# Two tiles in place of one for T's first place and the mixed weights, and 0.8 in place of 0.5 for a head's transfer

## The chip, the cores and the metric

The kernel runs on one core of a Trainium2 chip. Time is device time of one execution in microseconds (us); lower is better. A core has five engines with a queue of instructions each: TensorE (PE, its weight loads are shown as PEld), VectorE (DVE), ScalarE (ACT), GpSimd (POOL) and SyncE (SP), which here only starts DMA transfers. Each engine works through its queue in order and stands still when its next instruction waits.

## The reference

Attention over 4 batches, 12 heads, 448 tokens and 64 columns, in which the heads are mixed before and after the softmax, and then a two-layer network over the 1792 tokens:

```python
scores = scale * np.matmul(q, k.transpose(0, 1, 3, 2))
scores = np.einsum('bhij,hg->bgij', scores, w_pre)
scores = scores - np.max(scores, axis=-1, keepdims=True)
attn = np.exp(scores)
attn = attn / (np.sum(attn, axis=-1, keepdims=True) + 1e-09)
attn = np.einsum('bhij,hg->bgij', attn, w_post)
return np.matmul(attn, v).astype(np.float32)
...
h = x @ w_in
g = h * np.clip(h + 3.0, 0.0, 6.0) / 6.0
return (g @ w_out).astype(np.float32)
```

## The kernel before, in words

The tokens of a batch are taken in eight halves m of 60 (the last of a batch smaller), 32 halves in all. For a half, the products of q and k for 12 heads are made in three steps of four heads (`scores`, line 432). ScalarE copies each step's result from PSUM into one of two s buffers (line 457; the products go through one PSUM tile of two banks, `pair`). Then SyncE starts one transfer for each head (line 464), four for a step and twelve for a half (24 smaller ones in the last half of a batch). They turn the layout round: in T, the partitions are head and token, so that one matmul can mix the heads.

T has two places that alternate by half: even halves use the first 5376 columns of the tile AR, odd halves the tile T_one. From T the row products with w_pre are made (line 521), VectorE finds the maximum (529), ScalarE takes the exponential (530), GpSimd divides by the sum and splits the result into two 16-bit parts (539 to 542), and TensorE mixes the heads with w_post (558). Two engines write the mixed weights A into AR from column 6144 on: VectorE (567) and ScalarE (569). A has three slots in a ring there. From A and v come the attention outputs (603). The first layer of the network (801) fills in where it can, with its own evictions (814, 816). All of this is the first stage, to about 704 us; the second layer (1071) fills most of the rest. In the second stage AR holds weights and activations in two slots of 11520 columns (`wg`, `w_view`, `g_view`).

The order of all instructions is made ahead of time by a planner (`Plan`): each operation has an engine, an assumed time, what it reads and writes, and a priority; the planner plays the engines through, taking the operation of the best priority that is ready, tries 32 random variations and keeps the best. A DMA costs its engine the assumed time (0.5 for all of SyncE's), and lands later by its bytes. Where the plan sees TensorE idle near the start it puts matmuls without a result (line 839). The planner holds T's place and A for different buffers; the waits in the program are made afterwards, from tiles and what is read and written in them.

Of the kernel before, what the change touches and what calls it, by code (L numbers as in the profile page):

```python
# [11 lines left out]
F16 = mybir.dt.float16  # L12
BF16 = mybir.dt.bfloat16
F32 = mybir.dt.float32
# [12 lines left out]
P = 128  # L27
# [4 lines left out]
CU = 60  # L32
# [259 lines left out]
def body(ctx: ExitStack, tc: tile.TileContext, q4, kT, vj, wpre0, wpost0, ident0, w_in, w_out, outT):  # L292
    nc = tc.nc
    PE, ACT, DVE, POOL, SP = nc.tensor, nc.scalar, nc.vector, nc.gpsimd, nc.sync
# [4 lines left out]
    apool = ctx.enter_context(tc.tile_pool(name="apool", bufs=1))  # L299
# [9 lines left out]
    plan = Plan()  # L309
# [3 lines left out]
    def buf(pool, shape, dt, tag, name, bufs=1, ring=True):  # L313

        g = rings.setdefault((id(pool), tag), Ring(bufs)) if ring else None
        return Buf(lambda: pool.tile(shape, dt, tag=tag, name=name, bufs=bufs), g)

    def const(shape, dt, name, pool=keep):
        return Buf(lambda: pool.tile(shape, dt, name=name))

    def act(dur, fn, r, w, prio):
        return plan.op("ACT", dur, fn, r, w, prio)

    def dve(dur, fn, r, w, prio, share=False):
        return plan.op("DVE", dur, fn, r, w, prio, share=share)
# [4 lines left out]
    def pe(dur, fn, r, w, prio, after=(), mode=0):  # L330
        return plan.op("PE", dur, fn, r, w, prio, after, 0, mode)

    def dma(nbytes, fn, r, w, prio, after=()):
        return plan.op("SP", 0.5, fn, r, w, prio, after, nbytes)
# [22 lines left out]
    def place(places):  # L357
        z = Buf(None)
        z.pool = places
        return z  # L360
# [50 lines left out]
        qs[b, c] = t  # L411
        (bulk if b + c else dmas)(P * QX * 4, t, q4[b, c], [t], at, after)

    AR = const([P, 23424], F16, "AR", apool)
    T_one = const([P, 6, S], F32, "T_one", one)
    T_home = [lambda: AR()[:, :5376].bitcast(F32).rearrange("p (t j) -> p t j", t=6), T_one]
    T_zero = [Buf(None), T_one]
    a_ring = Ring(3)
    last_qk, last_av, Ts, Au = [], [], {}, {}

    def a_view():
        return AR()[:, 6144:].bitcast(F32).rearrange("p (x y) -> p x y", y=3 * CU)

    def products(q, half, ks_, p, at):

        def mm():
            for cc in range(2):
                pr = 2 * p + cc
                o = (6 * half + pr) * CU
                for u in range(2):  # L430
                    r = slice(u * D, u * D + D)
                    PE.matmul(at[u]()[cc * D:cc * D + D], q()[r, o:o + D], ks_[cc]()[r, pr % 3, :], start=True, stop=True)  # L432

        return mm

    def scores(m, p, at):
        b, n = divmod(m, 8)
        c, half = divmod(n, 2)
        if p == 0:
            Ts[m] = Buf(T_home[m % 2], rings.setdefault(("T", m % 2), Ring(1)))  # L440
        T, q = Ts[m], qs[b, c]
        ks_ = [ks[b, (2 * p + cc) // 3] for cc in range(2)]
        kr = [(ks_[cc], (2 * p + cc) % 3) for cc in range(2)]
        st = buf(wpool, [P, 2, S], F32, "x", f"s_{m}_{p}", X_BUFS) if m == 0 else buf(rot, [P, 2, S], F32, "s", f"s_{m}_{p}", 2)
        if m < 2 and (m or p):
            ps = [place(singles) for u in range(2)]
            at2 = [lambda u=u: ps[u]()[:, :S] for u in range(2)]
        else:
            two = place(pairs)
            ps = [(two, 0), (two, 1)]  # L450
            at2 = [lambda u=u: two()[:, u, :S] for u in range(2)]
        last_qk[:] = [pe(0.77, products(q, half, ks_, p, at2), [*kr, q], ps, at, last_qk, mode=1)]
        if m < 2:
            act(0.48, lambda: ACT.activation(st()[:, 0], at2[0](), AF.Copy), [ps[0]], [(st, 0)], at + 0.5)
            dve(0.57, lambda: DVE.tensor_copy(st()[:, 1], at2[1]()), [ps[1]], [(st, 1)], at + 0.5)
        else:
            act(0.9, lambda: ACT.activation(st(), two()[:, :, :S], AF.Copy), ps, [(st, 0), (st, 1)], at + 0.5)  # L457
        parts = [(0, 10, 6, 0)] if n < 7 else [(0, 10, 2, 0), (20, 5, 2, 2)]
        for cc in range(2):
            for u in range(2):  # L460
                h = 2 * (2 * p + cc) + u
                for q0, r, t, t0 in parts:
                    def go(cc=cc, u=u, h=h, q0=q0, r=r, t=t, t0=t0):
                        SP.dma_start(T()[4 + h:4 + h + 12 * (r - 1) + 1:12, t0:t0 + t], st()[D * cc + q0:D * cc + q0 + r * t, u, :])  # L464

                    dma(r * t * 2100, go, [(st, u), T_zero[m % 2]], [(T, (h, t0))], at + 0.7)


    vs = {}
# [32 lines left out]
    def step(s):  # L502
# [31 lines left out]
        if t == 0:  # L534
            Au[m] = Buf(a_view, a_ring)
# [312 lines left out]
    for m in range(2):  # L848
        for p in range(3):
            scores(m, p, -10 + 8 * m + 1.6 * p)  # L850
# [6 lines left out]
    for s in range(NS + 12):  # L857
# [5 lines left out]
        while todo and todo[0][0] - 2 <= s:  # L863
            at, m, p = todo.pop(0)
            if p == 0 and m % 2 == 0:
                queries(m // 8, m % 8 // 2, at - 5)
            scores(m, p, at)
# [13 lines left out]
        for C in range(16):  # L881
            b, c = divmod(C, 4)
# [28 lines left out]
    def minus(out, x, y, op, at, big, after=()):  # L911
        plan.op("DVE", 1.15, lambda: DVE.tensor_tensor(out(), x(), y(), op=op), [x, y], [out], at, after, share=True)

    WS, GP = {}, {}
    wg_ring = Ring(2)

    def wg(i):
        return Buf(lambda: AR()[:, 11520 * i:11520 * i + 11520], wg_ring)

    slots = [wg(i) for i in range(2)]  # L920
    t_last, a_last = last_pre[-5:-2], last_av[-4:]

    def w_view(t, z, i):
        return t()[:, :6144].rearrange("p (z m f c) -> p z m f c", z=2, m=3, f=8)[:, z, i // 2, 4 * (i % 2):4 * (i % 2) + 4]

    def g_view(t, at, z):
        return t()[:, at:at + 1792].rearrange("p (z f n) -> p z f n", z=2, f=4)[:, z]

    WS["P1"] = slots[0]

    def w_split(name, i, t, at, after):
        b = WS[name]
        split(View(t, lambda: t().rearrange("p (f c) -> p f c", f=4)), wo_r[int(name not in ("P1", "P2"))], lambda y: w_view(b, y, i), (b, (name, i)), 4 * P, at, after, False)

    def g_split(name, b, i, t, x, o, at, after):
        GP[name, b, i] = (lambda z: g_view(x, o, z)), (x, (name, b, i))
        split(t, g_s[b], lambda z: g_view(x, o, z), (x, (name, b, i)), 4 * NH, at, after, True)
# [69 lines left out]
    def g_tile(name):  # L1007
        return gbuf([P, 4, NH], F32, "gr", name, GR)

    def g_load(b, kk, half, i, at):  # L1010
        t = g_tile(f"g{kk}{half}_{b}_{i}_{at}")
        src, keys_ = g_rows(b, kk, half, i)
        load(458752, lambda: SP.dma_start(t(), src()), keys_, [t], at, [close_a])
        return t

    def g_put(name, b, i, t, at, home):
        after = [close_a]
        if home is None:
            ring = later_home.pop(0) if name not in ("P1", "P2") and later_home else "gx"
            if ring == "gy":  # L1020
                after = [close_a, close_w]
            x = gbuf([P, 1792], F16, "gx", f"gx_{name}_{b}_{i}", GX) if ring == "gx" else wbuf([P, 1792], F16, "gy", f"gy_{name}_{b}_{i}", GY)
            home = x, 0
        x, o = home
        g_split(name, b, i, whole(t), x, o, at, after + (a_last if x is slots[1] else []))
# [10 lines left out]
    def g_two(b, at):  # L1036
        later_home[:] = ["gy"] * GY
        if b % 2:
            z = [wg(i) for i in range(2)]
        for i in range(2):  # L1040
            t = at + (6 if b else G2_BY) * i
            b12, b11, b22, b21 = g_load(b, 0, 1, i, t), g_load(b, 0, 0, i, t + 0.1), g_load(b, 1, 1, i, t + 0.2), g_load(b, 1, 0, i, t + 0.3)
            t1 = g_tile(f"t1_{b}_{i}")
            minus(t1, b12, b11, ALU.subtract, t + 1, True)
            minus(b11, b22, t1, ALU.subtract, t + 1.1, True)
            minus(b12, b22, b12, ALU.subtract, t + 1.2, True)
            minus(b21, b21, b11, ALU.subtract, t + 1.3, True)
            for j, (name, x) in enumerate((("P6", b11), ("P7", b12), ("P4", b21), ("P5", t1), ("P3", b22))):
                home = None
                if b % 2:  # L1050
                    n = 5 * i + j
                    home = z[n // 5], 1792 * (n % 5)
                g_put(name, b, i, x, t + 2 + j, home)

    u_t = {}
# [78 lines left out]
    for b in range(B):  # L1134
        g_two(b, 2000 + 1000 * b if b else G2_AT)
        stage2(b, 20000 + 1000 * b)
# [54 lines left out]
```

## Time and profile before

| | |
|---|---|
| median of 3 runs | 926.43 us (920.86 to 934.22) |
| profiled execution | 935.05 us, span of its instructions 933.3 us |
| mean granted TensorE clock | 0.936 |
| TensorE busy | 838.6 us (90%) |
| VectorE, ScalarE, GpSimd busy | 602.5, 529.7, 373.1 us |

Busy time is the time in which at least one instruction of an engine ran. The granted clock is a share of full speed: 1.00 is 2.4 GHz, 0.50 is 1.2 GHz. A line such as "L567 DVE" is line 567 of the kernel on VectorE; `AR<-single` is the tile written and the tile read.

### The profile page before, as it was taken

How to read it: one execution, taken by the hardware profiler on the slowest of the kernel's cores; microseconds unless marked ns; L12 is line 12 of the kernel's file. 1: busy time of each engine (PE TensorE's matmuls, PEld its weight loads, DVE VectorE, ACT ScalarE, POOL GpSimd, SP SyncE). 2: the span in 40 equal slices, each digit the busy share in tenths (PEclk: the TensorE clock that was granted, in tenths of full speed). 3: DMA queues.
4: the chain of work that ended last, by engine and by line, in shares of the span. 5: the costliest groups of instructions: out<-in, count | busy, mean ns of one | idle time of the engine just before them, and what ended most of it. 6: DMA issues, size and time to landing. Idle time of an engine off the chain costs nothing.

```text
span 933.3 us, 28114 instructions
## 1 busy us (share of the span) xinstructions
PE 838.6 (90%) x11599; PEld 661.4 (71%) x11599; DVE 602.5 (65%) x1185; ACT 529.7 (57%) x1043; POOL 373.1 (40%) x535
## 2 busy tenths in 40 slices
PE   8699997698798898898897898889899999999998
PEld 2356665455475675676575666567799999999998
DVE  4477584458565734877565597586457588898542
ACT  3357685467676755676666666678447475243110
POOL 3145686267774744565545446668200000000000
PEclk9779699789999998999988999899999999999999
DMA  6563543362534465554645656553449785463301
GB/s 211 187 188 119 157 137 120 93 216 92 176 104 132 120 203 185 173 176 144 196 122 188 199 178 199 173 159 92 122 131 356 221 264 173 124 185 113 100 25 46
DMA packets 100417, 146.98 MB, mean 157 GB/s; under 512 B 9824, under 2 KB 79552, under 8 KB 100288
## 3 DMA queue, kind: packets, MB, share of 16 engines
q1 hardware_dynamic: 100288, 145.17, 50.1%
q8 instruction: 91, 1.49, 0.7%
q14 instruction: 38, 0.31, 0.1%
HBM read 75.23 MB, written 31.20 MB: 114 GB/s over the span
## 4 chain that ended last, share of the span: by engine, by line
PE 51%; DMA 12%; DVE 10%; ACT 8%; SPq 7%; POOL 6%; issue 5%; ACTq 0%; DVEq 0%; POOLq 0%
PE single L1071 21%; PE single L801 13%; SPq L464 6%; DMA AR<-s 6%; PE single L558 5%; PE pair L432 4%; PE single L521 3%; POOL e L539 3%; DVE nb L529 3%; POOL el L542 3%; PE single L603 2%; ACT e L530 2%; ACT s L457 2%; DMA T_one<-s 2%; DMA wsd_P<-WF 2%
## 5 line engine op out<-in xcount | busy, mean ns | idle before, releaser
L801 PEld LDWEIGHTS <-wi 128*128 128x128 f16 x2304 | 217.3, 99 | 37.1 <-issue 28.9
L801 PE MATMUL single<-x,wi 128*128 128x208 f16 (+1 forms) x2304 | 233.3, 263 | 9.4 <-ACT AR L569 6.6
L542 POOL TENSOR_TENSOR el<-e,eh 128x448 f16<-128x448 f32 x156 | 172.3, 1119 | 87.9 <-ACT eh L541 85.6
L539 POOL TENSOR_SCALAR e<-e,r 128x448 f32<-128x448 f32 x180 | 132.2, 746 | 77.1 <-DVE r L533 69.7
L1071 PEld LDWEIGHTS <-ws_P 128*128 128x128 f16 x1440 | 138.0, 98 | 0.0
L530 ACT ACTIVATE e<-single,nb 128x448 f32<-128x448 f32 x180 | 113.0, 637 | 35.2 <-DVE nb L529 34.9
L432 PE MATMUL pair<-ks,qx 64*64 64x448 f32 x728 | 101.6, 627 | 27.7 <-ACT s L457 27.3
L567 DVE TENSOR_SCALAR AR<-single 128x480 f32<-128x480 f32 (+1 forms) x92 | 58.4, 641 | 95.6 <-DMA AR<-s 68.7
L529 DVE TENSOR_REDUCE nb<-single 128x1 f32<-128x448 f32 x180 | 102.5, 613 | 21.9 <-PE single L521 21.6
L569 ACT ACTIVATE AR<-single 128x480 f32<-128x480 f32 (+1 forms) x92 | 52.9, 582 | 100.1 <-DMA AR<-s 66.5
L457 ACT ACTIVATE s<-pair 128x896 f32<-128x896 f32 x90 | 82.3, 915 | 37.6 <-DMA T_one<-s 20.6
L541 ACT ACTIVATE eh<-e 128x448 f16<-128x448 f32 x156 | 87.0, 576 | 19.8 <-POOL e L539 18.7
L814 ACT ACTIVATE g<-single,three,uh 128x240 f32<-128x240 f32 (+1 forms) x128 | 68.2, 540 | 51.6 <-PE single L801 51.2
L603 PEld LDWEIGHTS single<-AR,v 128*64 128x64 f32 x1536 | 80.6, 144 | 22.5 <-DVE AR L567 6.3
L558 PEld LDWEIGHTS <-eh 60*128 60x128 f16 x2496 | 69.2, 101 | 34.4 <-issue 31.2
L603 PE MATMUL single<-AR,v 128*64 128x120 f32 (+1 forms) x1536 | 86.1, 273 | 6.6 <-DVE AR L567 6.2
L816 DVE SCALAR_TENSOR_TENSOR g<-g,six,single 128x240 f32<-128x240 f32 (+1 forms) x128 | 56.3, 442 | 53.4 <-ACT g L814 53.1
L558 PE MATMUL single<-wpost_h,eh 60*128 60x60 f16 x1248 | 76.6, 204 | 11.1 <-ACT e L530 5.4
L558 PE MATMUL single<-wpost_h,el 60*128 60x60 f16 x1248 | 75.6, 204 | 4.4 <-POOL el L542 4.4
L558 PE MATMUL single<-wpost_l,eh 60*128 60x60 f16 x1248 | 75.4, 204 | 0.0
L1071 PE MATMUL single<-gx_P,ws_P 128*128 128x224 f16 x720 | 69.3, 259 | 0.0
L1071 PE MATMUL single<-AR,ws_P 128*128 128x224 f16 x720 | 69.3, 259 | 0.0
(241 smaller groups left out, 1163.8 us busy)
## 6 DMA issues: line engine op xcount, KB each, us to landing
AR<-s SPq DMA_DIRECT2D x192, 105.0 KB
T_one<-s SPq DMA_DIRECT2D x144, 105.0 KB
wi<-in_w_in SPq DMA_DIRECT2D x16, 768.0 KB
wo<-in_w_out SPq DMA_DIRECT2D x24, 512.0 KB
wsd_P<-WF SPq DMA_DIRECT2D x42, 256.0 KB
wP<-wsd_P SPq DMA_DIRECT2D x36, 256.0 KB
gd<-g SPq DMA_DIRECT2D x32, 240.0 KB
gd<-g SPq DMA_DIRECT2D x32, 208.0 KB
```

Of the source, the lines that this page charges most:

```text
L432: PE.matmul(at[u]()[cc * D:cc * D + D], q()[r, o:o + D], ks_[cc]()[r, pr % 3, :], start=True, stop=True)
L457: act(0.9, lambda: ACT.activation(st(), two()[:, :, :S], AF.Copy), ps, [(st, 0), (st, 1)], at + 0.5)
L529: dve(0.53, lambda r=r: DVE.tensor_reduce(nb()[:, r:r + 1], ps[r]()[:, :S], axis=AX.X, op=ALU.max, negate=True), [ps[r]], [(nb, r)], s + 0 ...
L530: act(0.62, lambda r=r: ACT.activation(e()[:, r], ps[r]()[:, :S], AF.Exp, bias=nb()[:, r:r + 1], accum_out=sm()[:, r:r + 1]), [ps[r], (nb, ...
L539: pool(0.63, lambda r=r: POOL.tensor_scalar(e()[:, r], e()[:, r], rr()[:, r:r + 1], 1.0, op0=ALU.mult, op1=ALU.mult), [rr], [(e, r)], s + ...
L541: act(0.47, lambda r=r: ACT.activation(eh()[:, r], e()[:, r], AF.Copy), [(e, r)], [(eh, r)], s + 0.65 + 0.3 * r)
L542: pool(1.02, lambda r=r: POOL.tensor_tensor(el()[:, r], e()[:, r], eh()[:, r], op=ALU.subtract), [(e, r), (eh, r)], [(el, r)], s + 0.7 + 0 ...
L558: PE.matmul(out, x()[rows, r, js], z()[rows], start=(i == 0), stop=(i == len(mix) - 1))
L603: PE.matmul(ps()[u * D:(u + 1) * D, k:k + (n if p1 else CI)], v()[:, jc, g * D:(g + 1) * D], cols(jc * H + g), start=(jc == 0), stop=(jc = ...
L801: PE.matmul(pv(), wi_g[g]()[:, w, f0, cc, :], x()[:, z, cc, :n], start=(cc == 0 and i == 0), stop=(cc == 5 and i == 2))
L814: act(0.44, lambda fc=fc, pv=pv, r=r: ACT.activation(r(), pv(), AF.Relu, bias=three()[:, fc:fc + 1], scale=uh()[:, fc:fc + 1]), [ps, (thre ...
L1071: PE.matmul(ps()[:, :NH], w_view(w, y, 2 * m + i)[:, f], g(x)[:, f, :], start=(i == 0 and f == 0 and (y, x) == (0, 0)), stop=(i == 1 and f ...
```

## The change

AR loses its first 6144 columns to a tile of its own, T_two, and A now begins at column 0 of AR. The second stage's two slots are made of pieces of both tiles; a tile's parts are found by `x[at // 6144]`, and of the ten places for g the third and later of a slot move by 768 columns. In the planner a head's transfer costs SyncE 0.8 in place of 0.5.

```diff
-    AR = const([P, 23424], F16, "AR", apool)
+    AR = const([P, 17280], F16, "AR", apool)
+    T_two = const([P, 6144], F16, "T_two", apool)
     T_one = const([P, 6, S], F32, "T_one", one)
-    T_home = [lambda: AR()[:, :5376].bitcast(F32).rearrange("p (t j) -> p t j", t=6), T_one]
+    T_home = [lambda: T_two()[:, :5376].bitcast(F32).rearrange("p (t j) -> p t j", t=6), T_one]
...
     def a_view():
-        return AR()[:, 6144:].bitcast(F32).rearrange("p (x y) -> p x y", y=3 * CU)
+        return AR()[:, :].bitcast(F32).rearrange("p (x y) -> p x y", y=3 * CU)
...
-                    dma(r * t * 2100, go, [(st, u), T_zero[m % 2]], [(T, (h, t0))], at + 0.7)
+                    plan.op("SP", 0.8, go, [(st, u), T_zero[m % 2]], [(T, (h, t0))], at + 0.7, (), r * t * 2100)
...
     def wg(i):
-        return Buf(lambda: AR()[:, 11520 * i:11520 * i + 11520], wg_ring)
+        return Buf(lambda: (AR()[:, 5376:11520], AR()[:, 11520:16896]) if i else (T_two(), AR()[:, :5376]), wg_ring)
...
     def w_view(t, z, i):
-        return t()[:, :6144].rearrange("p (z m f c) -> p z m f c", z=2, m=3, f=8)[:, z, i // 2, 4 * (i % 2):4 * (i % 2) + 4]
+        x = t()
+        return (x[0] if isinstance(x, tuple) else x[:, :6144]).rearrange("p (z m f c) -> p z m f c", z=2, m=3, f=8)[:, z, i // 2, 4 * (i % 2):4 * (i % 2) + 4]
 
     def g_view(t, at, z):
-        return t()[:, at:at + 1792].rearrange("p (z f n) -> p z f n", z=2, f=4)[:, z]
+        x = t()
+        if isinstance(x, tuple):
+            x, at = x[at // 6144], at % 6144
+        return x[:, at:at + 1792].rearrange("p (z f n) -> p z f n", z=2, f=4)[:, z]
...
-                    home = z[n // 5], 1792 * (n % 5)
+                    home = z[n // 5], 1792 * (n % 5) + (768 if n % 5 > 2 else 0)
```

Built with the two tiles alone, the program has every engine's instructions in the order of before, and only its waits differ; all that moves is moved by 0.8. The numbers in brackets below are semaphores: DMAHW0 to 7 are those of transfers, PE, DVE, Activation and Pool those of the engines.

VectorE, the first writes of A (line 567, in the change 568), near the start of the program; `vst` is a maximum over v, `WF` the decoding of weights. Before:

```order
L344 TENSOR_REDUCE vst_339<-v_266 128x1 [waits DMAHW0_49]
L567 TENSOR_SCALAR AR<-single_156 128x48x10 [waits DMAHW4_49,DMAHW5_49,DMAHW3_49,DMAHW6_49,DMAHW2_49,DMAHW7_49,DMAHW0_49,PE_49]
L533 RECIPROCAL r_375<-sm_337 128x2 [waits Pool_49]
L652 TENSOR_SCALAR WF,wist_380<-WF 128x768 [waits Activation_49]
L567 TENSOR_SCALAR AR<-single_139 128x48x10 [waits PE_49]
```

And with the change:

```order
L344 TENSOR_REDUCE vst_347<-v_299 128x1 [waits DMAHW6_49]
L568 TENSOR_SCALAR AR<-single_148 128x48x10 [waits PE_49]
L344 TENSOR_REDUCE vst_347<-v_299 128x1 [waits DMAHW7_49]
L534 RECIPROCAL r_372<-sm_315 128x2 [waits Pool_49]
L568 TENSOR_SCALAR AR<-single_85 128x48x10 [waits PE_49]
```

The first write of A waited for seven transfer semaphores and for TensorE; now only for TensorE.

ScalarE at the same place: line 457 (458) writes s, 569 (570) writes A, 530 (531) is the exponential. Before:

```order
L569 ACTIVATE AR<-single_147 128x48x10 [waits DMAHW6_49,DMAHW5_49,DMAHW7_49,DMAHW0_49,PE_49]
L649 ACTIVATE WF<-wi_276 128x768 [waits DMAHW1_49]
L569 ACTIVATE AR<-single_145 128x48x10 [waits PE_49]
L649 ACTIVATE WF<-wi_280 128x768 [waits DMAHW2_49]
L569 ACTIVATE AR<-single_85 128x48x10 [waits PE_49]
L457 ACTIVATE s_1_440<-pair_120 128x896 [waits Activation_49]
```

And with the change:

```order
L570 ACTIVATE AR<-single_146 128x48x10 [waits PE_49]
L570 ACTIVATE AR<-single_153 128x48x10 [waits PE_49]
L458 ACTIVATE s_1_395<-pair_120 128x896 [waits DMAHW1_49,DMAHW2_49,DMAHW0_49,DMAHW4_49,PE_49,Activation_49]
L531 ACTIVATE e_413,sm_414<-single_129,nb_405 128x448 [waits DVE_49,Pool_49]
L531 ACTIVATE e_413,sm_414<-single_138,nb_405 128x448 [waits DVE_49]
```

The transfers' semaphores went from the write of A to the write of s behind it.

SyncE around the last half of batch 0 (24 small transfers of s into T_one); `wi` are weights, `ks`, `qx` keys and queries, `gd` a store of the first layer. Before:

```order
L464 DMA AR<-s_1_1202 10x6x448 x4
L464 DMA AR<-s_2_1320 10x6x448 x4
L341 DMA wi_1375<-in_w_in 128x768
L819 DMA gd_1467<-g_0_1409 128x2x240
L819 DMA gd_1467<-g_2_1465 128x2x240
L341 DMA ks_0_1546<-in_kT 128x896
L341 DMA ks_0_1546<-in_kT 128x448
L464 DMA T_one<-s_0_1361 10x2x448
L464 DMA T_one<-s_0_1361 5x2x448 x2
L341 DMA ks_1_1623<-in_kT 128x448
L341 DMA ks_1_1623<-in_kT 128x896
L464 DMA T_one<-s_0_1361 5x2x448
```

And with the change:

```order
L465 DMA T_two<-s_2_1216 10x6x448 x4
L341 DMA wi_1274<-in_w_in 128x768
L341 DMA ks_0_1299<-in_kT 128x896
L341 DMA ks_0_1299<-in_kT 128x448
L820 DMA gd_1367<-g_0_1332 128x2x240
L341 DMA wi_1448<-in_w_in 128x768
L820 DMA gd_1367<-g_2_1389 128x2x240
L341 DMA ks_1_1482<-in_kT 128x448
L341 DMA ks_1_1482<-in_kT 128x896
L341 DMA qx_1_1518<-in_q 128x724
L341 DMA wi_1575<-in_w_in 128x768
L820 DMA gd_1367<-g_4_1542 128x2x240
```

All of the keys, one load of queries and two more of weights now stand ahead of the first of the 24 small transfers, which follow behind the last row.

## Rows read from the trace of the kernel before

**Rows 1.** The page, busy time (share of the span) and count by engine.
```profile
PE 838.6 (90%) x11599; PEld 661.4 (71%) x11599; DVE 602.5 (65%) x1185; ACT 529.7 (57%) x1043; POOL 373.1 (40%) x535
```

**Rows 2.** Two stretches: length, busy time (count) of PE, PEld, DVE, ACT, POOL, clock, DMA.
```profile
0.00:704.00 704.00, 612.48 (x9226) 435.84 (x9227) 446.31 (x954) 442.14 (x924) 372.76 (x533) 0.92 0.51 157
704.00:934.00 230.00, 226.16 (x2375) 225.57 (x2373) 156.17 (x232) 87.53 (x120) 0.33 (x2) 1.00 0.50 157
```

**Rows 3.** The page, chain of work that ended last, by engine and by line.
```profile
PE 51%; DMA 12%; DVE 10%; ACT 8%; SPq 7%; POOL 6%; issue 5%; ACTq 0%; DVEq 0%; POOLq 0%
PE single L1071 21%; PE single L801 13%; SPq L464 6%; DMA AR<-s 6%; PE single L558 5%; PE pair L432 4%; PE single L521 3%; POOL e L539 3%; DVE nb L529 3%; POOL el L542 3%; PE single L603 2%; ACT e L530 2%; ACT s L457 2%; DMA T_one<-s 2%; DMA wsd_P<-WF 2%
```

**Rows 4.** Waits: who waited for whom, total us, times, longest.
```profile
DVE AR L567 <- DMA AR<-s: 68.7, 18, 13.5
ACT AR L569 <- DMA AR<-s: 66.5, 20, 10.9
...
PE pair L432 <- ACT s L457: 27.3, 15, 4.6
...
ACT s L457 <- DMA T_one<-s: 20.6, 10, 4.8
...
PE single L521 <- DMA T_one<-s: 4.2, 3, 2.5
```

**Rows 5.** Waits of SyncE's queue.
```profile
SPq L464 <- DVE AR L567: 37.9, 18, 5.5
```

**Rows 6.** Timeline, 154 to 177 us: start, length, engine, line, operation [idle before <- releaser].
```profile
154.23 3.90 SPq L464 DMA_DIRECT2D T_one<-s  x4
...
159.26 3.18 SPq L464 DMA_DIRECT2D AR<-s  x4
...
163.10 11.13 SPq L464 DMA_DIRECT2D AR<-s  x4
169.51 0.66 DVE L567 TENSOR_SCALAR AR<-single 128x480 f32<-128x480 f32 x1 [13.53 <-DMA AR<-s]
...
170.22 5.07 PE L603 MATMUL single<-AR,v 128*64 128x120 f32 x48 [6.20 <-DVE AR L567]
...
172.87 0.59 ACT L569 ACTIVATE AR<-single 128x480 f32<-128x480 f32 x1 [10.91 <-DMA AR<-s]
```

**Rows 7.** The stretches with a write of A waiting for a transfer; columns of rows 2.
```profile
29.40:37.90 8.50, 3.47 (x46) 2.54 (x44) 1.68 (x3) 0.00 (x0) 1.45 (x3) 0.90 0.85 297
...
622.70:624.70 2.00, 0.58 (x7) 0.43 (x5) 1.08 (x1) 0.00 (x0) 0.28 (x1) 1.00 0.35 102
sum 87.50, PE 57.81 PEld 39.45 DVE 15.93 ACT 8.78 POOL 28.56; mean PE 2.63 PEld 1.79 DVE 0.72 ACT 0.40 POOL 1.30
```

**Rows 8.** Six stretches at half clock; columns of rows 2.
```profile
36.20:46.50 10.30, 7.05 (x41) 4.61 (x41) 5.39 (x10) 4.01 (x6) 1.25 (x2) 0.50 0.28 75
...
589.20:596.00 6.80, 5.44 (x68) 3.42 (x69) 5.80 (x14) 6.02 (x13) 2.84 (x5) 0.50 0.24 67
sum 51.30, PE 35.81 PEld 21.47 DVE 26.44 ACT 27.62 POOL 14.79; mean PE 5.97 PEld 3.58 DVE 4.41 ACT 4.60 POOL 2.46
```

**Rows 9.** Line 464: duration ns min/median/max, first and last start.
```profile
L464 SPq DMA_DIRECT2D T_one<-s x240: 712/749/1506, 17.3 to 652.3; - x120
L464 SPq DMA_DIRECT2D AR<-s x192: 748/749/1797, 7.2 to 622.0; - x192
```

**Rows 10.** The chain in order of time, 286 to 306 us: start, length, what.
```profile
290.19 3.55 DMA AR<-s
```

**Rows 11.** Timelines of 110 to 135 and 315 to 334 us.
```profile
116.23 2.68 PE L603 MATMUL single<-AR,v 128*64 128x120 f32 x48
...
326.95 3.15 SPq L464 DMA_DIRECT2D AR<-s  x4
```

**Rows 12.** Groups of instructions by line and shape: count, busy us, mean ns, idle before.
```profile
L839 PE MATMUL single<-ident 128*128 128x512 bf16 x63 | 18.3, 434 | 0.1
```

## Prediction, before the changed kernel had run

> **What bounds the kernel now.** I read the busy line first. TensorE is busy for 838.6 of 933.3 us [rows 1], which looks like a kernel with no room. The stretches say where that is true. The attention stage, 0 to 704 us, has 612.48 us of TensorE work at a mean granted clock of 0.92, so 91.5 us are idle; the stage after it has 226.16 of 230.00 at clock 1.00 [rows 2]. The diff's places are all in the first stage, or are columns of the second that are read as before, so whatever is won or lost comes out of the first 704 us. Next the chain that ended last: 6% of the span is "DMA AR<-s", 6% is SyncE issuing at line 464, and only 2% is "DMA T_one<-s" [rows 3]. T's two places are filled by the same code, yet the one inside AR costs three times the other. The waits say why: VectorE stands 68.7 us and ScalarE 66.5 us in front of their writes of A (lines 567 and 569) until a transfer into AR has landed [rows 4]. Those writes go to columns 6144 and up of AR, the transfers to columns below 5376. No byte is shared, and no such wait stands in front of the halves whose T is T_one. SyncE has the mirror of it: 37.9 us in 18 times before a transfer until a VectorE write of A is over [rows 5].
>
> One place shows the whole effect. From 156.0 us VectorE stands still for 13.53 us, ScalarE for 10.91, until the transfers issued from 159.26 on have landed; TensorE runs dry for 6.20 us behind it [rows 6].
>
> **The change, part by part.**
>
> *Waits removed.* In the order, 36 of 92 writes of A on VectorE and 33 of 92 on ScalarE wait for DMA queues before; after, none. I laid the 38 waits over each other: they make 22 stretches of 87.50 us together, in which TensorE is busy 57.81 [rows 7]. So 29.7 us of TensorE's idle time stand directly inside them. I take all of it: **-29.7 us**. The bounds are 0 (something else is late at the same moment) and -87.5 (the whole chain moves up by it).
>
> *Clock.* Six stretches at granted clock 0.50, the 1.2 GHz level, begin in or right behind such a wait: 51.30 us with 35.81 us of TensorE work [rows 8]. What half clock costs shows on one group: the 48 matmuls of line 603 take 5.07 us there [rows 6] and 2.68 at full clock [rows 11]. If all six went, half of 35.81 would, 17.9 us. Other gaps remain that can lower the clock, so I take half: **-9**, between 0 and -17.9.
>
> *SyncE freed.* Of the transfers into T's first place, 35 wait for VectorE before, 3 after. Held transfers hold the s buffers, and TensorE waits 27.3 us for s to be emptied [rows 4]. The 37.9 us [rows 5] are mostly cover for waits of A itself, already counted; I price them by TensorE's share of idle time inside waits (29.7 of 87.5, 0.34), and half of that: **-6**, between 0 and -13.
>
> *A wait that takes the place of the removed one.* The write of s (line 457) must wait until the s buffer two tiles earlier is read out. Before, 50 of its 90 instructions say so; the other 40 stood behind a write of A that had waited already. After, 90 of 90 do. Behind this instruction in ScalarE's queue stand the exponentials, and TensorE's next products need the pair it empties. Its price is in the halves that have it already: 20.6 us in 10 times for T_one [rows 4]. The other halves should pay the same, and a 0.34 of it reaches TensorE: **+7**, between 0 and +20.6.
>
> *Other order.* The split moves no instruction; the number 0.8 moves all of them. One issue of a head's transfer takes 749 ns on SyncE [rows 9], so the plan was short by 0.25 us in each of 432 issues, 108 us in all, and is now over by 0.05. Worst was the last half of a batch, with 24 small issues: 18 us on the queue where the plan saw 12, and just there the 13.53 us wait begins. A truer plan keeps s tiles further apart; it also has 98 idle-time matmuls where there were 63, at 0.29 us each (18.3 over 63 [rows 12]) 10 us, which lie where the plan sees TensorE idle. If that cover is missing they cost those 10 us. I take **-4**: half of the 7 us that 20.6 us of T_one waits cost TensorE by the same 0.34, between -15 and +15, since a reshuffled order can go either way. The Trainium skill, "DMA: Bandwidth & Descriptors", section "Issuing engines are not separate DMA queues", says that the sequencer's time to start a DMA is usually small relative to the DMA itself, and by it this term is 0 and the sum 4 us smaller. The trace does not agree: four issues fill 3.15 us of the queue [rows 11], and a landing awaited behind them took 3.55 [rows 10].
>
> *Second stage.* The weights and g's lie in the same number of columns, in two pieces; no wait there is added or removed on TensorE: **0**, while it is at 226.16 of 230.00 us [rows 2].
>
> Sum: -29.7 - 9 - 6 + 7 - 4 = **-42 us**. As a cross-check, if T's first place came to cost the chain what T_one does, 6% would become 2%, 37 us of 933.3 [rows 3]. The profiled execution took 935.05 us, 8.6 above the median of 926.43, so it goes to 893; against the median, **884 us**.
>
> **Rivals.**
>
> *More than the sum* (chance 0.15, about 865). All of the clock comes back (17.9) and the s waits shrink with SyncE's load instead of doubling: 29.7 + 17.9 + 13 = 61 us. For it: the chain has 12% in the AR transfers and line 464's issues [rows 3]. Against: 62 of the 91.5 idle us stand outside the removed waits.
>
> *The wait comes back at s* (0.15, about 912). If the 40 newly waiting writes of s stand as long as the writes of A did, ScalarE keeps 66.5 us instead of 20.6, and 0.34 of the difference, 16 us, returns, with the clock's 9 and half of SyncE's 6: of the 42, 14 us are left. For it: the transfers themselves are not shortened. Against: a write of A waited for twelve transfers of a half, s waits for the four of one tile.
>
> *TensorE is simply full* (0.06, 926). Its matmuls cover 87% of the stage; then what stops VectorE and ScalarE, 63% busy each, moves nothing, because TensorE's queue has work ahead. For it: in the 22 stretches TensorE is busy two thirds of the time [rows 7]. Against: 29.7 us in them are idle. The Trainium skill, "Perfetto Trace Analysis", section "Identifying the Most-Contended Engine", says to improve the engine with the highest occupancy first, which here is TensorE and which this change does not touch; the same section warns that matmul busy time is a poor measure, and weight loads fill only 435.84 of the 704 us [rows 2].
>
> *Slower: T comes too late* (0.07, about 964). With dearer transfers the planner spreads a half's twelve over a longer stretch and puts other loads between them, and SyncE is one queue in order. TensorE's first row product of a half (line 521) then waits for the last landing, with everything behind it. It does so 3 times now, up to 2.5 us [rows 4]. At 2.5 us in each of 32 halves it is 80 us against 42 won, 38 slower. It passes the 18.5 us bound from 60/32 = 1.9 us per half. Against: at a true 0.75 us the plan sees the landing better than it did at 0.5.
>
> **From cases to numbers.** The forecast has 0.57. Two per cent of 926, which is 18.5 us, is about what a measurement of this kernel can tell from no change. Faster by more than that is under 908: the forecast, the larger case and a third of the s case, 0.77. Within it: two thirds of the s case and the full TensorE, 0.16. Slower, over 945: 0.07. The forecast's terms alone span about 870 to 900; 860 to 914 takes in the s case and most of the larger one and leaves out the slow case, no change and the far end of the larger.
>
> **What would show it.** In the changed profile: no wait of the A writes for a DMA; "DMA T_two<-s" near 2% of the chain; TensorE idle in the first stage down from 91 to about 60 us and that stage's clock above 0.92; the s write's wait for DMA at about 40 us in all; line 464's successor with no VectorE wait. I am wrong on the s term if that wait is near 65 us, on the order if the row products wait over 20 us for T, and on the whole if the first stage still ends near 700.

## The result, and the profile after

The changed kernel takes **815.21 us** (811.8 to 817.13, 4 runs) against 927.13 for the kernel before: a ratio of 0.8787, 95% interval 0.8716 to 0.8857. It was forecast to be faster, at 884 us and not under 860: the sign is right, and 112 us were won where 42 were forecast.

The busy line of the changed kernel's page (busy us, share of the span, count), to set beside [rows 1]:

```profile
PE 791.4 (97%) x11634; PEld 639.0 (79%) x11634; DVE 599.9 (74%) x1185; ACT 529.6 (65%) x1043; POOL 376.7 (46%) x535
```

The span went from 933.3 to 812.6, by 120.7 us. TensorE's idle time fell from 94.7 to 21.2 and its busy time, for the same products and 35 more idle-time matmuls, from 838.6 to 791.4: 73.5 us of idle time and 47.2 us of slower work. Two stretches, cut where the second layer's matmuls begin, against [rows 2] (length, busy time of PE, PEld, DVE, ACT, POOL, granted clock, DMA share, GB/s):

```profile
0.00:613.00 613.00, 594.87 (x9583) 442.73 (x9584) 453.12 (x974) 452.58 (x945) 376.35 (x533) 0.99 0.60 185
613.00:813.00 200.00, 196.54 (x2053) 196.28 (x2052) 146.76 (x212) 77.00 (x99) 0.33 (x2) 1.00 0.53 169
```

The second stretch is 30 us shorter only because 323 matmuls of the first layer, 30 us of work, that lay behind the cut before now lie ahead of it; its idle time is 3.5 us where it was 3.8. The first stage's idle time is 18 us where it was 91.5, and its mean clock is 0.99. One stretch at half clock is left, between 28.1 and 38.3 us, where there were fifteen of 119.5 us together; here with its busy times (same columns):

```profile
28.10:38.30 10.20, 10.20 (x71) 6.03 (x73) 4.02 (x6) 2.90 (x4) 2.55 (x5) 0.50 0.79 259
```

The chain that ended last, by engine and by line, against [rows 3]:

```profile
PE 62%; DMA 9%; ACT 8%; POOL 6%; DVE 6%; SPq 5%; issue 3%; ACTq 0%; POOLq 0%; DVEq 0%
PE single L1076 24%; PE single L802 16%; PE single L559 6%; PE pair L433 5%; SPq L465 4%; PE single L522 4%; PE single L604 4%; ACT e L531 3%; POOL el L543 2%; POOL e L540 2%; DMA T_two<-s 2%; PE single L840 2%; DMA wi<-in_w_in 2%; ACT s L458 2%; DMA wo<-in_w_out 2%
```

T's first place has gone from 6% to 2%, as the cross-check had it, and the issues of a head's transfers from 6% to 4%. The waits, against [rows 4] (who waited for whom, us in total, times, longest):

```profile
PE pair L433 <- ACT s L458: 3.2, 6, 0.7
...
ACT s L458 <- DMA T_two<-s: 6.7, 5, 2.3
...
ACT s L458 <- DMA T_one<-s: 4.1, 5, 2.0
```

No write of A waits for a transfer. The wait at the write of s, forecast at 40 us, is 10.8. And the place of [rows 6], behind the small transfers of batch 0's last half (timeline: start, length, engine, line, operation [idle before <- releaser]):

```profile
134.29 4.04 SPq L465 DMA_DIRECT2D T_one<-s  x5
135.45 2.68 PE L604 MATMUL single<-AR,v 128*64 128x120 f32 x48
...
138.41 0.58 ACT L570 ACTIVATE AR<-single 128x480 f32<-128x480 f32 x1
138.54 3.15 SPq L465 DMA_DIRECT2D T_two<-s  x4
...
141.73 0.66 DVE L568 TENSOR_SCALAR AR<-single 128x480 f32<-128x480 f32 x1 [1.49 <-PE single L559]
```

A is written while T's transfers are on their way, and the 48 matmuls of line 604 take 2.68 us where they took 5.07.

### The profile page after: what moved, and what is told of

The parts are those of the page before. It is cut to its first block, busy times and chain, and to the rows that moved or that the text cites. A ratio compares the mean times of both kernels' runs of the same rounds, so it can differ in the third digit from the quotient of the medians.

```text
span 812.6 us, 28101 instructions
## 1 busy us (share of the span) xinstructions
PE 791.4 (97%) x11634; PEld 639.0 (79%) x11634; DVE 599.9 (74%) x1185; ACT 529.6 (65%) x1043; POOL 376.7 (46%) x535
## 4 chain that ended last, share of the span: by engine, by line
PE 62%; DMA 9%; ACT 8%; POOL 6%; DVE 6%; SPq 5%; issue 3%; ACTq 0%; POOLq 0%; DVEq 0%
PE single L1076 24%; PE single L802 16%; PE single L559 6%; PE pair L433 5%; SPq L465 4%; PE single L522 4%; PE single L604 4%; ACT e L531 3%; POOL el L543 2%; POOL e L540 2%; DMA T_two<-s 2%; PE single L840 2%; DMA wi<-in_w_in 2%; ACT s L458 2%; DMA wo<-in_w_out 2%
## 5 line engine op out<-in xcount | busy, mean ns | idle before, releaser
L802 PEld LDWEIGHTS <-wi 128*128 128x128 f16 x2304 | 213.0, 98 | 22.7 <-issue 14.1
L802 PE MATMUL single<-x,wi 128*128 128x208 f16 (+1 forms) x2304 | 227.6, 259 | 2.8 <-ACT e L531 2.2
L543 POOL TENSOR_TENSOR el<-e,eh 128x448 f16<-128x448 f32 x156 | 176.0, 1145 | 36.6 <-ACT eh L542 33.3
L433 PE MATMUL pair<-ks,qx 64*64 64x448 f32 x728 | 89.3, 560 | 3.7 <-ACT s L458 3.2
L815 ACT ACTIVATE g<-single,three,uh 128x208 f32<-128x208 f32 (+1 forms) x128 | 68.7, 539 | 37.1 <-PE single L802 35.5
L817 DVE SCALAR_TENSOR_TENSOR g<-g,six,single 128x208 f32<-128x208 f32 (+1 forms) x128 | 56.4, 442 | 44.8 <-ACT g L815 42.9
L604 PEld LDWEIGHTS single<-AR,v 128*64 128x64 f32 x1536 | 75.1, 137 | 13.4 <-issue 3.4
L604 PE MATMUL single<-AR,v 128*64 128x120 f32 (+1 forms) x1536 | 80.4, 263 | 0.4 <-ACT e L531 0.4
L533 POOL TENSOR_SCALAR sm<-sm 128x2 f32<-128x2 f32 (+1 forms) x92 | 21.8, 237 | 106.3 <-ACT e L531 101.4
L559 PEld LDWEIGHTS <-el 60*128 60x128 f16 x1248 | 64.1, 101 | 2.5 <-POOL el L543 2.4
```

The lines of the kernel that those rows point to most:

```text
L543: pool(1.02, lambda r=r: POOL.tensor_tensor(el()[:, r], e()[:, r], eh()[:, r], op=ALU.subtract), [(e, r), (eh, r)], [(el, r)], s + 0.7 + 0 ...
L559: PE.matmul(out, x()[rows, r, js], z()[rows], start=(i == 0), stop=(i == len(mix) - 1))
L604: PE.matmul(ps()[u * D:(u + 1) * D, k:k + (n if p1 else CI)], v()[:, jc, g * D:(g + 1) * D], cols(jc * H + g), start=(jc == 0), stop=(jc = ...
L802: PE.matmul(pv(), wi_g[g]()[:, w, f0, cc, :], x()[:, z, cc, :n], start=(cc == 0 and i == 0), stop=(cc == 5 and i == 2))
L815: act(0.44, lambda fc=fc, pv=pv, r=r: ACT.activation(r(), pv(), AF.Relu, bias=three()[:, fc:fc + 1], scale=uh()[:, fc:fc + 1]), [ps, (thre ...
```

## The experiments

Two theories stood first. **W**: the removed waits carry the gain. **P**: the truer plan carries it. The two parts of the change fall apart cleanly: the tiles change waits and no order, the number moves the order. The traces bear this out: in the kernel before and in e1 every engine starts the same lines in the same order, and so it does in e2 and in the changed kernel (a few matmuls that run side by side apart).

**e1, two tiles alone**

```diff
-                    plan.op("SP", 0.8, go, [(st, u), T_zero[m % 2]], [(T, (h, t0))], at + 0.7, (), r * t * 2100)
+                    dma(r * t * 2100, go, [(st, u), T_zero[m % 2]], [(T, (h, t0))], at + 0.7)
```

> Two tiles alone, 0.5 kept: every engine's order is that of the kernel before, only the waits of the A writes for transfers are gone. Theory W (the waits carry it: each idle stretch of TensorE breeds half-clock time and later idle time, so removing them is worth two to three times the 29.7 us that stand inside them): 825 to 855 us, half-clock time under 30 us, TensorE idle in the first stage about 30 us. Theory P (the plan carries it: the waits are worth the 42 us that I priced, the rest comes from counting 0.8): 875 to 890 us, half-clock time about 70 us.

875.16 us against 928.46 (ratio 0.9445, 0.9404 to 0.9485): 53 us. Its busy line, and its first 650 us (columns of [rows 2]):

```profile
PE 815.5 (94%) x11599; PEld 652.6 (75%) x11599; DVE 600.7 (69%) x1185; ACT 530.4 (61%) x1043; POOL 374.4 (43%) x535
...
0.00:650.00 650.00, 596.67 (x9302) 434.32 (x9303) 451.57 (x969) 450.00 (x936) 374.37 (x535) 0.94 0.55 174
```

Idle time is 56.5 us of its span of 872.0 and busy time 815.5: 38 us of idle time and 23 of slower work came back. The time lies 20 us above W's range, and of the first 650 us 53.3 are still idle where W had about 30. So in the order of before the waits are worth less than half of the 112 us. P gets its number for this half, at the very edge of its range, with its half-clock time (about 72 us by the mean clock of 0.959), though 53 is more than the 38 that my terms for the tiles make.

**e2, 0.8 alone**, in the kernel before:

```diff
-                    dma(r * t * 2100, go, [(st, u), T_zero[m % 2]], [(T, (h, t0))], at + 0.7)
+                    plan.op("SP", 0.8, go, [(st, u), T_zero[m % 2]], [(T, (h, t0))], at + 0.7, (), r * t * 2100)
```

> 0.8 alone, one tile kept: the order of the changed kernel with the false waits of the kernel before. Theory W: within 15 us of before, 912 to 940 us, the A writes wait for transfers about as long as before (65 us on each of VectorE and ScalarE). Theory P: 850 to 885 us. If neither half is worth much alone and only both together are, both this and the two tiles alone stay above 880 us.

907.04 us (0.9769, 0.9708 to 0.9829): 21 us, outside the ranges of both theories, and by its interval not clear of 2%. Its busy line and its waits (same columns as above):

```profile
PE 836.8 (92%) x11634; PEld 656.1 (72%) x11634; DVE 599.3 (66%) x1185; ACT 529.8 (58%) x1043; POOL 372.2 (41%) x535
...
ACT AR L569 <- DMA AR<-s: 102.3, 29, 8.6
DVE AR L567 <- DMA AR<-s: 85.5, 25, 8.2
```

The waits of the writes of A are longer than before, 187.8 us in all where they were 135.2 [rows 4]. The plan knows nothing of them, so the order cannot avoid them. From e2 to the changed kernel, with every instruction in the same order, 92 us go: the same removal of waits is worth 53 us in the old order and 92 in the new one, and the number is worth 21 us with those waits in place and 60 without them. Apart the two halves make 74 of the 112 us, and 38 come only with both, so neither W nor P describes the gain. This holds for the one order that each number gave; one tile was not drawn again, and a re-deal of the order moves the time by up to 25 us (below), so the 38 are no general figure.

**e3, e6: two tiles, 0.5, other draws; e5, e7: the changed kernel, the same draws.** The number moves every instruction, so its effect could be luck. The draw is the seed of the planner's variations, 1000 in e3 and e5, 2000 in e6 and e7:

```diff
-            rnd = random.Random(k)
+            rnd = random.Random(k + 1000)
```

> Two tiles, 0.5, and the planner's 32 random variations drawn from other seeds: how far a mere re-deal of the order moves the time. If 0.8 is worth something as a truer number, this lies within 8 us of the two tiles alone; if any re-deal moves the time by 20 us or more, the part that 0.8 plays cannot be told from luck by one order.

> The changed kernel (two tiles, 0.8) with the planner's variations drawn from other seeds, those of e3. Theory N (0.8 is a truer number and any draw with it is better): 805 to 830 us, against 849.7 for 0.5 with the same draw. Theory L (luck: orders scatter by some 30 us whatever the number, and 815 is a good draw): anywhere from 825 to 865 us.

> Two tiles, 0.5, a third set of draws. Theory N: 845 to 880 us, like the two draws known (875.2 and 849.7). Theory L: it may fall anywhere from 815 to 880 us.

> Two tiles, 0.8, the third set of draws (that of e6). Theory N: 805 to 830 us and at least 20 us under e6. Theory L: no fixed side to e6.

| draw | two tiles, 0.5 | two tiles, 0.8 | difference |
|---|---|---|---|
| first | 875.16 | 815.21 | 60 |
| second | 849.66 | 825.54 | 24 |
| third | 863.80 | 825.57 | 38 |

A re-deal moves 0.5 by up to 25 us and 0.8 by 10. The time of e5 lies in the ranges of both theories; what decides is that 0.8 is ahead in all three draws, by 41 us on average, and that its slowest draw is 24 us ahead of the fastest of 0.5. So it is the number (N), and by this average some 20 of the 60 us in the change's own draw are luck.

**e8, e9, e10, e11, e15: other numbers** in `plan.op("SP", 0.8, go, ...)` of the changed kernel; e15 is 1.1 with the second draw:

```diff
-                    plan.op("SP", 0.8, go, [(st, u), T_zero[m % 2]], [(T, (h, t0))], at + 0.7, (), r * t * 2100)
+                    plan.op("SP", 1.1, go, [(st, u), T_zero[m % 2]], [(T, (h, t0))], at + 0.7, (), r * t * 2100)
```

> Two tiles, and 1.1 for a head's transfer, above the 0.75 us that the trace shows. If what counts is that the plan is true, 1.1 is as far over as 0.5 is under and costs 15 us or more: 830 to 860 us. If what counts is that the plan is never short (slack in SyncE's queue), it is as good as 0.8: 810 to 825 us.

> Two tiles, 0.65. The step from one issue of a head's transfer to the next is 0.80 us in the trace (749 ns of the instruction and some 50 between). If the time follows how far the plan is short of the step, this lies halfway between the draws with 0.5 (850 to 875) and those with 0.8 (815 to 826): 828 to 850 us, with the s write's wait for transfers between the 10.8 us of the changed kernel and the 28 us of 0.5.

> Two tiles, 0.75, the duration of the instruction without the 50 ns that follow. If the plan only has to be about right, 812 to 832 us, no different from 0.8 by more than a re-deal makes (10 us).

> Two tiles, 0.95. If over-counting is what makes 1.1 slow, and smoothly so: 835 to 865 us, halfway to 888.6, with an s wait under 8 us and more TensorE idle time than the 18 us of the changed kernel. If 1.1 was one bad draw: 812 to 832 us.

> Two tiles, 1.1, with that draw. If over-counting by 0.3 us an issue costs by itself: 860 to 900 us, with next to no wait at the write of s. If the 888.6 us of e8 were a bad draw: 815 to 840 us, as with 0.95.

| number | 0.5 | 0.65 | 0.75 | 0.8 | 0.95 | 1.1 |
|---|---|---|---|---|---|---|
| us | 850 to 875 | 849.56 | 833.68 | 815 to 826 | 826.17 | 884.67, 888.55 |

0.65 fell within its range, at the upper end, with an s wait of 21.4 us between the two as expected. 0.75 is 1.7 us outside what I expected, 8 us above the slowest draw of 0.8; with one draw it cannot be told from 0.8 by more than a re-deal. 0.95 is as good as 0.8 within a re-deal, against the smooth rise of one of its two expectations. 1.1 is bad in both draws, and e8 is above both of its ranges. The kernel before took 922.35 us beside 0.65, 0.75 and 0.95, and 927 to 930 beside the others; scaled by it to 927.13 these three are 854, 838 and 830 us (an estimate), and 0.65 is 4 us above its range. The best numbers, 0.8 and 0.95, cannot be told apart. 0.8 is the step that SyncE really takes, as the chain of the kernel before shows it (start, length, what):

```profile
117.40 0.75 SPq L464
118.15 0.05 issue
118.20 0.75 SPq L464
```

From issue to issue it is 0.80 us: the prediction took the 749 ns of [rows 9] for it, and left out the 0.05.

**e13, e14: what carries it.** The plan may take the s buffers for free too early (S), or what stands behind the heads' transfers in SyncE's queue may come too late (Q). Here the queue is counted at 0.5 again and only the landing is later (e14 with the second draw):

```diff
-                o.end = bw[e] + 1.9
+                o.end = bw[e] + (3.1 if o.mode == 9 else 1.9)
...
-                    plan.op("SP", 0.8, go, [(st, u), T_zero[m % 2]], [(T, (h, t0))], at + 0.7, (), r * t * 2100)
+                    plan.op("SP", 0.5, go, [(st, u), T_zero[m % 2]], [(T, (h, t0))], at + 0.7, (), r * t * 2100, 9)
```

> Two tiles, 0.5 for the queue, but the plan lets a head's transfer land 1.2 us later (3.1 in place of 1.9 behind its bytes), which is what four issues short by 0.3 us each make for the last of a tile. Theory S (the carrier is the s buffer: the plan takes it for free too early, writes of s block ScalarE and TensorE behind them): most of the gain of 0.8, 815 to 840 us, s wait under 16 us. Theory Q (the carrier is SyncE's queue: loads and other transfers that stand behind the heads' transfers come later than planned): 845 to 880 us as with 0.5, s wait above 20 us or other waits for DMA in its place.

> As before, with the draw of e3 and e5: theory S 815 to 840 us, theory Q 840 to 880 us; 849.7 is 0.5 with this draw and 825.5 is 0.8.

859.74 and 851.41 us: no better than 0.5 beyond a re-deal. Three waits views show why; first two tiles alone (e1):

```profile
ACT s L458 <- DMA T_one<-s: 17.8, 12, 4.1
DVE WF L755 <- DMA wsd_P<-WF: 12.7, 5, 3.6
DVE vst L344 <- DMA v<-in_vj: 12.0, 5, 5.1
ACT s L458 <- DMA T_two<-s: 10.2, 9, 2.7
ACT WF L650 <- DMA wo<-in_w_out: 9.4, 3, 3.7
ACT WF L650 <- DMA wi<-in_w_in: 6.4, 3, 3.2
```

With the later landing (e13):

```profile
ACT WF L650 <- DMA wo<-in_w_out: 24.6, 10, 8.7
DVE WF L755 <- DMA wsd_P<-WF: 12.7, 3, 6.4
DVE vst L344 <- DMA v<-in_vj: 10.6, 7, 4.3
ACT s L458 <- DMA T_one<-s: 9.0, 8, 2.7
ACT WF L650 <- DMA wi<-in_w_in: 8.3, 5, 3.2
...
ACT s L458 <- DMA T_two<-s: 0.9, 1, 0.9
```

And the changed kernel:

```profile
ACT WF L650 <- DMA wo<-in_w_out: 7.5, 7, 1.7
...
DVE WF L755 <- DMA wsd_P<-WF: 6.0, 3, 3.0
...
ACT WF L650 <- DMA wi<-in_w_in: 2.9, 2, 2.0
DVE vst L344 <- DMA v<-in_vj: 2.6, 4, 1.6
```

Theory S got what it asked for, the s wait down from 28.0 to 9.9 us, and the time stayed. The waits for weights, v and stores, whose transfers share the queue, went up, from 40.5 to 56.2: with those of s the six rows sum to 68.5 us in e1, 66.1 in e13, 29.8 in the changed kernel. The other draws say the same: 54.6 and 55.3 us in e3 and e6 with 0.5, 62.7 in e14, 29.9 and 27.8 in e5 and e7 with 0.8. And the sum falls with the number all the way: 39.4 at 0.65, 33.2 at 0.75, 15.2 at 0.95, 11.4 and 10.2 at 1.1. Only counting the queue itself moves all of them. S is out as the carrier, and Q fits every one of these runs; that the lateness of the whole queue costs the time is argued from the waits, since no run delays the queue with the order held.

What makes 1.1 slow is another thing. In e8 few waits for DMA are left and TensorE is idle for 61.5 us again, 22 of them between 600 and 800 us, where the changed kernel has next to none; the queue stands and waits for the engines, over 20 us each where the changed kernel has 4.9 and 9.5 us for the same two (waits of SyncE's queue in e8):

```profile
SPq L465 <- ACT s L458: 22.5, 13, 5.0
SPq L465 <- ACT AR L570: 21.0, 13, 5.6
```

That fits an order laid out for a queue that is busier than it is; why it sets in between 0.95 and 1.1 was not taken apart.

**e4, no idle-time matmuls**, in the changed kernel:

```diff
-    FILL_FROM, FILL_TO = 9, 150
+    FILL_FROM, FILL_TO = 9, 9
```

> The changed kernel without the 98 matmuls without a result that the plan puts into TensorE's expected idle time. If they are what keeps the clock at 1.00 from 38 us on: half-clock time rises to 40 us or more and the time to 830 to 840 us. If the clock is kept by the work itself: one or two more half-clock stretches before 165 us, time within 6 us of 815.

814.94 us (0.8792, 0.8750 to 0.8835 of before; the changed kernel 0.8787). Its busy line has 11.7 us less TensorE work than the changed kernel's, and the time is the same:

```profile
PE 779.7 (96%) x11536; PEld 635.7 (78%) x11536; DVE 602.1 (74%) x1185; ACT 530.1 (65%) x1043; POOL 377.1 (46%) x535
```

Mean clock is 0.977 in place of 0.994: six half-clock stretches, 37.5 us, are there where one was, all before 166 us, and from there on the work keeps the clock at 1.00 by itself. The time is that of the second expectation, the half-clock time comes near the 40 us of the first. In the changed kernel the 98 matmuls take 24.8 us of TensorE's time. Without them its busy time fell by only 11.7, so the rest of the work took about 13 us longer, and its idle time rose by 13.3, from 21.2 to 34.5: the two together eat up what was spared. The 35 more of these matmuls that the plan with 0.8 has are therefore not what carries the gain.

**e12, 96 draws in place of 32**:

```diff
-TRIALS, JITTER = 32, 0.3
+TRIALS, JITTER = 96, 0.3
```

> The changed kernel, with 96 in place of 32 random variations tried by the planner (the first 32 are the same). If the plan with 0.8 is true enough that its own best is the chip's best, this is as fast or faster: 800 to 817 us. If what is left between plan and chip is as large as a re-deal, it lies anywhere within 805 to 828 us.

815.90 us: the same as with 32 and within the ranges of both expectations, so no version was found that beats the changed kernel.

## Why the prediction was right and wrong

*Right.* The gain is in the first stage alone; the second is 196.54 of 200.00 us busy, as idle as before and at clock 1.00 in both. The writes of A waited for bytes that they do not share, and do so no longer. The s wait did not take the place of the A waits (28.0 us in e1, against 20.6 in half the halves before), and T does not come too late for the row products.

*The step that failed: the other order, at -4 us between -15 and +15.* It measures -21 with the one tile, -60 with two tiles in this draw and -41 on average over three. I had the ingredients: 432 issues counted short, by 0.3 us each rather than the 0.25 that I took. I then priced the lateness only by the wait whose row names T_one, 20.6 us, and by the share that reached TensorE. But SyncE is one queue in order, so what stands behind a late issue is late too: in e13 the waits for weights, v and stores rise as those of s fall, and the time stays within a re-deal. Such rows, filed under other names, were in the same waits view before, if smaller than they became in e1:

```profile
DVE WF L754 <- DMA wsd_P<-WF: 10.6, 4, 4.9
...
ACT WF L649 <- DMA wo<-in_w_out: 4.8, 2, 4.1
```

Also I took the re-deal for symmetric, between ends that were no measurement: re-deals with 0.5 alone span 25 us. The Trainium skill ("DMA: Bandwidth & Descriptors", "Issuing engines are not separate DMA queues") says that the sequencer's time to start a DMA is usually small relative to the DMA itself. Here one issue takes 0.75 us [rows 9] and a landing 3.55 [rows 10], but four issues fill 3.15 us of the queue [rows 11], and 0.3 us in the plan's count of an issue was worth 41 us on average.

*The sum itself.* I priced each term in the kernel before and added them up. The two halves do not add: 38 of the 112 us come only with both, which no term and no rival had.

*The clock, at -9 and never beyond -17.9.* Right in kind, far too small: with the idle time the busy time fell by 47.2 us, 23.1 of them in e1. I let only the six stretches in or right behind a removed wait come back. In the changed kernel fourteen of fifteen are gone, also those with no such wait near; the idle time of the whole stage went with them, from 91.5 to 18 us.

*The removed waits, at -29.7.* The term was near: e1 has 38 us less idle time, which holds the waits, SyncE's freedom and the s wait together, where mine sum to -28.7. Removing them was worth 53 us, clock included, in place of 38, and 92 in the new order.

*The rival "more than the sum"* named the right direction and stopped too early, at 865. Its argument against, that 62 us of idle time stand outside the removed waits, was the mistake in short: idle time that no row ties to the edit is not thereby out of its reach when the edit moves every instruction.

## What to carry to other kernels

When a planner orders the work, compare each cost it assumes with the step from one such instruction to the next in the trace, the queues' own too; an error on a queue that all transfers share can delay every transfer behind it, and then shows in the waits view under all their names. A wait that the planner does not know of undoes part of a truer plan (here the number won 21 us with such waits in place and 60 without), so mend both together. And before calling a new order better, draw it several times: here one draw was worth up to 25 us.

## What was not expected of the hardware

TensorE's time at half clock went with its idle time: 119.5 us at half clock and 94.7 idle before, about 72 and 56.5 in e1, 37.5 and 34.5 in e4, 10.2 and 21.2 after. Two pairs of runs have the same matmuls in the same order and differ by the waits alone. From before to e1, 38.2 us of idle time went and 23.1 us of slower work with it, 0.60 us for each; from e2 to the changed kernel 48.7 and 45.4, or 0.93. So a removed wait gave back much more than TensorE's idle time, but at no fixed rate.
